# Two token blocks of the first layer by a Strassen form, and attention tiles turned by two VectorE transposes

## The chip, the cores and the metric

The kernel runs on one core of one Trainium2 chip. The metric is the device time of one execution in microseconds, the median of the runs.

## The reference

Attention in chunks of 64 tokens, then two feed-forward layers, all in float32 (cut to what matters):

```python
# q, k, v: (4, 8, 576, 64); chunks of 64 tokens that see only themselves
scores = matmul(q_c, k_c.T) / sqrt(64)
attn = exp(scores - max) / (sum + 1e-9)
x = (attn @ v_c), heads side by side          # (2304, 512)
h = x @ w_in1                                 # (2304, 2048)
g = softplus(h);   x = g @ w_out1             # (2304, 512)
h = x @ w_in2
g = (a0 + a1 h + a2 h^2 + a3 h^3) / (1 + |b0||h| + |b1| h^2 + 1e-6)
out = g @ w_out2
```

## The kernel before

**Number form.** A float32 product is made of three matmuls: each operand is split into a high part (rounded for the matmul, written by ScalarE or GpSimd) and a rest (`lo`, a subtraction on VectorE or GpSimd), and high x high, high x rest and rest x high are added in PSUM. The tuple `TERMS` holds the three. A weight tile or an x tile holds both parts, index 0 and 1.

**Tiles.** A *feature group* (`fc`) is 128 of the 2048 hidden features, 16 in all. A *block* is a set of tokens: layer one has 512, 512, 512, 384 and 384 (`BLOCKS`, blocks 0 to 4), layer two 512, 512, 512, 512 and 256. For one block and one group, `products_h` issues 12 matmuls (4 pieces of the 512 inputs x 3 terms) into a PSUM bank of `ps_h`, which has two; `softplus` (ScalarE twice, then the rest) or `rational` (six VectorE and five ScalarE instructions, and the rest on GpSimd) makes g, and `products_out1` or `products_out2` adds g times W_out into four banks for the whole block, 12 matmuls in two halves. The matmuls of h stand on L959, those of out on L1163 and L1196.

**Order of the blocks.** Layer one goes through blocks 0, 3, 4, 1, 2 (`ORDER1`), one group after another; layer two through 0, 3, 4, 1, 2 of its own.

**Attention.** A tile is 128 tokens, 18 in all. Seven are `STAGED` (0 to 3 and 12 to 14) and stand ready at the start in room that weights take later: PE turns q and k for them (`transpose`). The other eleven are loaded while layer one runs, with q and k in one tile of the pool `raw`, two transfers for most, and turned by 16 VectorE instructions of 32 partitions x 256 (`turn_blocks`, L655); their e is turned by 8 such instructions (`turn_e_blocks`, L759). PE adds 16 small matmuls for the scores (L677) and 16 for the values (L775). `finish_attention` lets the values of one tile go together with the scores of the next.

**Weights.** A 512 KB piece of a weight comes through SP's queue into `raw` (four buffers, shared with the attention), ScalarE and VectorE put it into float32 (`convert`: a scaling, a shift, one or two merges), and it is split into parts. Layer one's 32 pieces are converted during block 0. For layer two, 16 are converted early, stored to DRAM and loaded again (`reload_w`), and the `DIRECT` ones are converted when they are needed.

**Order of the work.** Every step is a task of `Program` with its engine, a cost, the tiles it reads and writes and the pool tags that it takes; the planner simulates these costs backward and forward, shakes the order and keeps the best one, and the program is written out in that order. Each engine then goes through its own instructions in order, SP through its transfers.

Of the kernel before, what the change touches and what calls it, by code (L numbers as in the profile page):

```python
# [20 lines left out]
P = 128  # L21
CH = 64
# [4 lines left out]
ORDER1 = (0, 3, 4, 1, 2)  # L27
# [4 lines left out]
DIRECT = range(2, 10)  # L32
# [6 lines left out]
APART = (0, 3)  # L39
PIECES = ((0, 256), (256, 256))  # L40
STAGED = (0, 1, 2, 3, 12, 13, 14)
QK_BY_VECTOR = {*range(4, 12), *range(15, 18)}
E_BY_VECTOR = {*range(4, 12), *range(15, 18)}


DIVIDE_BY_POOL = ()


FIRST_LOADS = "q0 k0 q1 k1 q2 k2 q3 k3 v0 v1 i0 v2 v3 i1 o0 q12".split()


class Program:
# [15 lines left out]
    def __init__(self):  # L68
        self.tasks, self.deps, self.table, self.port, self.psum = [], [], [], [], []
        self.writer, self.readers, self.last_alloc = {}, {}, {}  # L70
# [17 lines left out]
    def add(  # L88
# [22 lines left out]
        self.tasks.append((engine, cost, fn))  # L111
        self.deps.append(deps)
# [113 lines left out]
    def schedule(self):  # L226
# [7 lines left out]
        for seed in range(self.SEEDS):  # L234
# [48 lines left out]
def tile_chunk_attention_two_ffn(  # L283
# [72 lines left out]
    def on_dve(n, pointers=0):  # L356
        return 0.07 + 0.06 * pointers + n / 960

# [58 lines left out]
    def prepare(name, after, signed):  # L417
        layer, which, fc = name
        rkey = turn("raw", 4)
        spare = layer == 1 and turn("spare", 4)[1] == 3  # L420
# [84 lines left out]
    def reload_w(which, fc):  # L505
        if fc in DIRECT:
            convert(2, [(which, fc)], after=[steps[-1]])
            return
# [25 lines left out]

    loads = {}
# [5 lines left out]
    unfinished, done, begin = [], {}, {}  # L541

# [7 lines left out]
    def attention(tb):  # L550
# [13 lines left out]

        def load_qk(n):
# [3 lines left out]
            def f():  # L569
                if not staged and n == 0:  # L570
                    shape = [P, H, 2, D] if qk_by_vector else [P, 2, H, D]
                    qk_t[tb] = raw.tile(shape, F32, tag="raw", name=f"qk_{tb}")
                for off, m, b, s in runs(tb * TB, TB):
                    if not qk_by_vector:
# [4 lines left out]
                        continue  # L579
                    p0 = 64 * n + off // 2  # L580
                    sync.dma_start(
                        out=qk_t[tb][p0 : p0 + m // 2].rearrange("p h t d -> p h (t d)"),
                        in_=(q, k)[n][b, :, s : s + m, :].rearrange(
                            "h (p t) d -> p h (t d)", t=2
                        ),
                    )
# [3 lines left out]
        def load_v():  # L590
            if not staged:
                v_t[tb] = att1.tile([P, H, D], F32, tag="v", name=f"v_{tb}")
            for off, m, b, s in runs(tb * TB, TB):
# [54 lines left out]
        def turn_blocks(n, c, h, dq):  # L648


            def f():
                if (n, c, h, dq) == (0, 0, 0, 0):
                    new_turned()
                p0, p1 = 64 * h + 32 * dq, 64 * n + 32 * c
                vec.transpose(  # L655
                    tiles["qkT"][p0 : p0 + 32, n, :, c * CH : (c + 1) * CH].rearrange(
                        "p g (u t) -> p g t u", t=2
                    ),
                    qk_t[tb][p1 : p1 + 32, h::2, :, 32 * dq : 32 * dq + 32],
                )  # L660
# [3 lines left out]
        def scores():  # L664

            if qk_by_vector:
                new_ps()
            for n in range(16):
                g, c = (n // 4, n // 2 % 2) if by_chunk else (n // 8 * 2 + n // 2 % 2, n // 4 % 2)
# [825 lines left out]
```

## Time and profile before

| | |
|---|---|
| median of three runs (lowest, highest) | 842.61 us (842.59, 842.86) |
| span of the profiled execution | 842.7 us |
| PE busy | 832.9 us, 99% |
| VectorE, ScalarE, GpSimd busy | 639.7, 499.7, 226.0 us |
| chain that ended last | 97% PE |

The span is the time from the first to the last instruction of the one execution that was profiled; it stands beside the runs, which were not profiled. An engine's busy time says how much it did, the chain which of it was waited for. The granted clock is TensorE's, as a share of its full 2.4 GHz.

### The profile page before, as it was taken

The numbers are of one execution on the slowest core, as the hardware profiler recorded it, in microseconds if no ns is written. First come the engines' busy times: TensorE is split into PE (matmuls) and PEld (weight loads), VectorE is DVE, ScalarE is ACT, GpSimd is POOL, SyncE is SP. The second block draws the span as 40 slices with busy tenths as digits, with TensorE's granted clock in tenths as the row PEclk, the third lists the DMA queues.
The fourth block names the chain that finished last, engine by engine and source line by source line (L and its number), as shares of the span: only waits on it lengthen the run. The fifth ranks groups of instructions, "written<-read, shape, count | busy, mean of one in ns | idle before, by whom it ended". The sixth has DMA issues, their size and how long they took to land.

```text
span 842.7 us, 13146 instructions
## 1 busy us (share of the span) xinstructions
PE 832.9 (99%) x5020; PEld 714.7 (85%) x5020; DVE 639.7 (76%) x1125; ACT 499.7 (59%) x869; POOL 226.0 (27%) x206
## 2 busy tenths in 40 slices
PE   7999999999999999999999999999999999999998
PEld 6888889999999888888888888888889888888886
DVE  5788687887989887218887876868788886796785
ACT  5899962323335333244449766766778875676674
POOL 0000002222222121244355822322226261321312
PEclk9899999999999999999999999999999999999999
DMA  9965424214443713255434100200021000001001
GB/s 213 269 208 179 171 64 127 49 38 138 138 114 100 201 39 113 88 168 167 152 100 137 39 1 1 76 0 1 1 88 64 0 26 1 1 7 44 1 1 51
DMA packets 77984, 71.11 MB, mean 84 GB/s; under 512 B 36192, under 2 KB 65376, under 8 KB 77920
## 3 DMA queue, kind: packets, MB, share of 16 engines
q1 hardware_dynamic: 77920, 70.27, 28.8%
q8 instruction: 39, 0.64, 0.3%
q14 instruction: 25, 0.20, 0.1%
HBM read 56.63 MB, written 13.63 MB: 83 GB/s over the span
## 4 chain that ended last, share of the span: by engine, by line
PE 97%; SPq 2%; DMA 1%; ACT 0%; issue 0%
PE h L959 47%; PE acc L1163 24%; PE acc L1196 23%; PE aps L775 1%; SPq L575 1%; DMA wr_1i<-in_moe_w_in_dram 1%; PE aps L677 1%; PE h L984 1%; SPq L594 0%; SPq L427 0%; PE aps L630 0%; PE aps L746 0%; ACT cm_1i L446 0%; ACT ev_last L1262 0%; ACT room L768 0%
## 5 line engine op out<-in xcount | busy, mean ns | idle before, releaser
L1163 PE MATMUL acc<-g,w_1o 128*128 128x512 f32 (+1 forms) x960 | 210.9, 369 | 0.0
L959 PE MATMUL h<-xT,w_2i 128*128 128x512 f32 (+1 forms) x960 | 207.8, 368 | 0.0
L1196 PE MATMUL acc<-w_2o,g 128*128 128x512 f32 x864 | 206.6, 389 | 0.0
L959 PE MATMUL h<-xT,w_1i 128*128 128x512 f32 (+1 forms) x948 | 206.2, 368 | 0.0
L959 PEld LDWEIGHTS h<-xT,w_2i 128*128 128x128 f32 x960 | 168.9, 188 | 31.3 <-ACT u L1066 0.3
L1163 PEld LDWEIGHTS acc<-g,w_1o 128*128 128x128 f32 x960 | 174.1, 188 | 22.8
L959 PEld LDWEIGHTS h<-xT,w_1i 128*128 128x128 f32 x948 | 172.3, 188 | 22.2
L1196 PEld LDWEIGHTS acc<-w_2o,g 128*128 128x128 f32 x864 | 161.3, 188 | 32.8
L1034 POOL TENSOR_TENSOR g<-t,g 128x384 fp32r<-128x384 f32 (+1 forms) x64 | 76.5, 1196 | 325.8 <-ACT g L1031 325.8
L1099 POOL TENSOR_TENSOR g<-t,g 128x512 fp32r<-128x512 f32 (+1 forms) x80 | 94.6, 1183 | 253.6 <-ACT g L1096 169.2
L1026 ACT ACTIVATE t<-h 128x512 f32<-128x512 f32 (+1 forms) x80 | 44.5, 556 | 113.7 <-PE h L959 113.5
L1031 ACT ACTIVATE g<-h 128x512 fp32r<-128x512 f32 (+1 forms) x80 | 44.5, 556 | 73.4 <-PE acc L1163 71.8
L655 DVE STREAM_TRANSPOSE qkT<-qk 32x256 f32<-32x256 f32 x176 | 76.9, 437 | 12.0 <-PE aps L677 8.1
L1069 DVE SCALAR_TENSOR_TENSOR t<-u,absb_t,t 128x512 f32<-128x512 f32 (+1 forms) x80 | 55.5, 694 | 26.3 <-ACT u L1066 15.1
L1125 DVE TENSOR_TENSOR t<-h,t 128x512 f32<-128x512 f32 (+1 forms) x80 | 50.8, 636 | 31.5 <-ACT t L1084 14.4
L1114 ACT ACTIVATE t<-h,na_t 128x512 f32<-128x512 f32 (+1 forms) x80 | 58.6, 733 | 18.0 <-PE h L959 15.8
L1096 ACT ACTIVATE g<-t 128x512 fp32r<-128x512 f32 (+1 forms) x80 | 46.8, 585 | 37.7 <-DVE t L1069 34.6
L1069 DVE SCALAR_TENSOR_TENSOR t<-t,epsq_t,u 128x512 f32<-128x512 f32 (+1 forms) x80 | 55.3, 691 | 13.9 <-ACT u L1092 13.6
L1088 ACT ACTIVATE u<-t,epsq_t 128x512 f32<-128x512 f32 (+1 forms) x80 | 51.8, 648 | 22.6 <-DVE t L1069 20.5
L1069 DVE SCALAR_TENSOR_TENSOR t<-t,na_t,h 128x512 f32<-128x512 f32 (+1 forms) x80 | 55.5, 693 | 10.8 <-ACT t L1084 5.3
L1084 ACT ACTIVATE t<-h,b_t 128x512 f32<-128x512 f32 (+1 forms) x80 | 51.3, 641 | 16.8 <-PE h L959 10.1
L1069 DVE SCALAR_TENSOR_TENSOR u<-t,na_t,u 128x512 f32<-128x512 f32 (+1 forms) x80 | 55.6, 696 | 0.0
(86 smaller groups left out, 725.2 us busy)
## 6 DMA issues: line engine op xcount, KB each, us to landing
wr_1i<-in_moe_w_in_dram SPq DMA_DIRECT2D x16, 512.0 KB, 4.1
wr_1o<-in_moe_w_out_dram SPq DMA_DIRECT2D x16, 512.0 KB, 4.8
wr_2i<-in_moe_w_in_dram SPq DMA_DIRECT2D x16, 512.0 KB, 4.2
wr_2o<-in_moe_w_out_dram SPq DMA_DIRECT2D x16, 512.0 KB, 3.9
qk<-in_q_dram SPq DMA_DIRECT2D x16, 256.0 KB, 4.9
qk<-in_k_dram SPq DMA_DIRECT2D x16, 256.0 KB, 5.2
v<-in_v_dram SPq DMA_DIRECT2D x16, 256.0 KB, 5.0
out_dram<-ev SPq DMA_DIRECT2D x16, 256.0 KB, 2.5
```

The source lines that it names most:

```text
L655: vec.transpose(tiles["qkT"][p0 : p0 + 32, n, :, c * CH : (c + 1) * CH].rearrange("p g (u t) -> p g t u", t=2), qk_t[tb][p1 : p1 + 32, h:: ...
L959: pe.matmul(hs[s], w[:, a, c * P : (c + 1) * P], xt[:, b, c, :n_tok], start=n == 0, stop=n == 3 * KC - 1,)
L1034: (vec if by_vector else pool).tensor_tensor(out=gs[s][:, 1, :n_tok], in0=t["t2"], in1=gs[s][:, 0, :n_tok].bitcast(F32), op=ALU.subtract,)
L1069: return lambda: vec.scalar_tensor_tensor(out=out(), in0=in0(), scalar=scalar, in1=in1(), op0=op0, op1=op1)
L1084: act.activation(new("t1"), h(), AF.Abs, scale=b_t[:, 0:1])
L1088: act.activation(u(), d(), AF.Ln, bias=epsq_t)
L1096: act.activation(gs[s][:, 0, :n_tok], p(), AF.Copy)
L1099: pool.tensor_tensor(out=gs[s][:, 1, :n_tok], in0=p(), in1=gs[s][:, 0, :n_tok].bitcast(F32), op=ALU.subtract,)
L1114: lambda: act.activation(new("t2"), h(), AF.Identity, scale=na_t[:, 3:4], bias=na_t[:, 2:3]),
L1125: lambda: vec.tensor_tensor(out=p(), in0=h(), in1=p(), op=ALU.mult), [hkey, kp], [kp],
L1163: pe.matmul(accs[1, j, half][c % 2][:, :n_tok], wts[1, "o", fc][:, a, c * P : (c + 1) * P], gs[s][:, b, :n_tok], start=first and n == 0, s ...
L1196: pe.matmul(accs[2, j, half][c % 2], gs[s][:, b, c * P : (c + 1) * P], wts[2, "o", fc][:, a, :], start=first and n == 0, stop=last and n == 2,
```

## The change

**Order.** Layer one goes through blocks 0, 1, 2, and then through 3 and 4 together (`PAIR`). The staged tiles are 0 to 6; tile 7 comes during block 0, tiles 8 to 12 during block 1 and 13 to 17 during block 2.

**The pair.** For two feature groups f1, f2 and the two blocks a, b the four products h = x times W_in form a 2 x 2 matrix product, with the 512 inputs in halves: A11, A12 (group f1, inputs 0 to 255 and 256 to 511), A21, A22 (group f2), B11, B21 (block a) and B12, B22 (block b). `pair` forms S1 = A21 + A22, S2 = S1 - A11, S3 = A11 - A21, S4 = A12 - S2 on VectorE and splits them into parts; `turned_operands` and `turned_late` form, tile by tile, T1 = B12 - B11, T2 = B22 - T1, T3 = B22 - B12, T4 = T2 - B21. Seven products of 256 inputs (2 pieces x 3 terms = 6 matmuls) then stand where eight stood, with Winograd's order of sums: some of them in PSUM, where a later product goes on in a bank that ScalarE (`take`) or VectorE (`plus`) has read. Softplus of block a gives g as before; g of block b is kept in the room of used W_in tiles, and the out products of block b follow when all eight pairs are done.

**Attention.** q and k of a tile come in 16 transfers of 32 tokens x 8 heads x 32 values, so that one VectorE transpose of 128 x 512 turns q and one turns k (`turn_blocks`); v comes in four. GpSimd divides e for tiles 7 to 17.

**Weights of layer two.** `DIRECT` is 0 to 7; the reloads begin under block b's out products (`BACK`), and the direct ones are converted with one merge instead of two.

```diff
-ORDER1 = (0, 3, 4, 1, 2)
+ORDER1 = (0, 1, 2)
+PAIR = (3, 4)
-DIRECT = range(2, 10)
+DIRECT = range(0, 8)
-STAGED = (0, 1, 2, 3, 12, 13, 14)
+STAGED = tuple(range(7))
+BEGUN = (1, 5, 5)
+BEGIN_AT = ((9,), (0, 3, 6, 9, 13), (0, 2, 4, 7, 9))
+CONVERT = ((), (1, 2, 4, 5, 7, 8, 10, 11, 12, 14, 15), (1, 2, 3, 4, 5))
+BACK = (0, 0, 1, *(1,) * 13)
-DIVIDE_BY_POOL = ()
+DIVIDE_BY_POOL = range(7, 18)
+PAIR_BY_VECTOR = ("S24", "S1", "S3", "C12", "C22")
...
+                for c, b, s in chunks():
+                    for d0 in range(0, D, 32):
+                        for t0 in range(0, CH, 32):
+                            p0 = CH * c + d0
+                            sync.dma_start(
+                                out=qk_t[tb][p0 : p0 + 32, n, :, t0 : t0 + 32],
+                                in_=(q, k)[n][
+                                    b, :, s + t0 : s + t0 + 32, d0 : d0 + 32
+                                ].rearrange("h p d -> p h d"),
+                            )
...
-        def turn_blocks(n, c, h, dq):
+        def turn_blocks(n):
...
                 vec.transpose(
-                    tiles["qkT"][p0 : p0 + 32, n, :, c * CH : (c + 1) * CH].rearrange(
-                        "p g (u t) -> p g t u", t=2
-                    ),
-                    qk_t[tb][p1 : p1 + 32, h::2, :, 32 * dq : 32 * dq + 32],
+                    tiles["qkT"][:, n].rearrange("p g t -> p (g t)"),
+                    qk_t[tb][:, n].rearrange("p h t -> p (h t)"),
                 )
...
+    def turned_operands(part):
...
+            add(DVE, on_dve2(512), whole, [((xa, i), 0), ((xa, i), 1)], [ka], alloc="t1", port=True)
+            add(DVE, on_dve2(256), t3, [km], [kt], alloc="t1", port=True)
+            add(DVE, on_dve2(256), t1, [km, ka, kt], [km], port=True)
+            add(DVE, on_dve2(256), t2, [km, ka], [ka], port=True)
...
+    def pair(pi, s):
...
+        add(DVE, on_dve2(512), whole(f2), [(w2, 0), (w2, 1)], [k2], alloc="t1", port=True)
+        add(DVE, on_dve2(512), whole(f1), [(w1, 0), (w1, 1)], [k1], alloc="t1", port=True)
+        add(DVE, on_dve2(256), combine((f2, 1), (f2, 0), (f2, 1), ALU.add), [k2], [k2], port=True)
+        add(DVE, on_dve2(256), combine((f2, 0), (f1, 0), (f2, 0), ALU.subtract), [k1, k2], [k2], port=True)
+        add(DVE, on_dve2(256), combine((f1, 0), (f2, 1), (f1, 0), ALU.subtract), [k1, k2], [k1], port=True)
+        add(DVE, on_dve2(256), combine((f1, 1), (f1, 1), (f1, 0), ALU.subtract), [k1], [k1], port=True)
...
+        def product(a, b, n, new, start):
+            def f():
+                if new:
+                    new_bank(n)
+                for m, (i, j, c) in enumerate((i, j, c) for i, j in TERMS for c in range(2)):
+                    pe.matmul(
+                        banks[n], lhs(a, i, c), right(b, j, c),
+                        start=start and m == 0, stop=m == 5, skip_group_check=not start,
+                    )
...
+        def take(name):
...
+                act.activation(t[name], banks[0], AF.Copy)
...
+        def plus(name, k):
...
+                vec.tensor_tensor(out=t[name], in0=banks[1], in1=t[name], op=ALU.add)
...
+        product("A11", "B11", 0, True, True)
+        k11 = take("u1")
+        product("A12", "B21", 1, True, True)
+        plus("u1", k11)
+        g11 = activate("u1", k11, "A", f1, s + f1)
+        product("S2", "T2", 0, False, False)
+        k12 = take("u2")
+        product("S1", "T1", 1, False, True)
+        product("S3", "T3", 0, False, False)
+        k22 = take("u3")
+        plus("u3", k22)
+        product("A22", "T4", 0, False, False)
+        g21 = activate(None, None, "A", f2, s + f2)
+        product("S4", "B22", 1, False, False)
+        plus("u2", k12)
+        g12 = activate("u2", k12, "B", f1, s + FC + f1)
+        g22 = activate("u3", k22, "B", f2, s + FC + f2)
```

What this does to the order of the instructions is shown at three places. The first is PE in the stage of blocks 3 and 4. Before, in block 4, h of a group (12 matmuls into `h`) and the halves of out (into `acc`) take turns:

```order
L959 MATMUL h_36_2389<-xT_1693,w_1i_128 128x384 x12
L959 MATMUL h_37_2409<-xT_1693,w_1i_129 128x384 x12
L1163 MATMUL acc_4_1_0_2353<-g_2373,w_1o_648 128x384 x3
L1163 MATMUL acc_4_1_1_2354<-g_2373,w_1o_648 128x384 x3
L1163 MATMUL acc_4_0_2316<-g_2373,w_1o_648 128x384 x6
```

Now, in the fifth pair, the same place reads so (`p_0` and `p_1` are the pair's two banks; `s_4` holds S2 and S4, `S_4_3848` is S1, `S_4_3891` is S3; `T_0_3236` and `T_1_3237` are the two parts of T2, `T_0_3233` and `T_1_3234` those of T3; `xT_3366` holds T1):

```order
L1453 MATMUL p_0_3816<-T_1_3237,s_4_3921 128x384 x2
L1453 MATMUL p_0_3816<-T_0_3236,s_4_3921 128x384 x2
L1453 MATMUL p_1_3829<-xT_3366,S_4_3848 128x384 x6
L1453 MATMUL p_0_3816<-T_0_3233,S_4_3891 128x384 x2
L1453 MATMUL p_0_3816<-T_1_3234,S_4_3891 128x384 x2
```

Between S2 times T2 and S3 times T3, both into `p_0`, stands one group of six matmuls, S1 times T1; `take("u2")` on ScalarE reads `p_0` in that time.

The second place is SP's queue in the middle of block 0 (`wr_1i`, `wr_1o` are pieces of layer one's W_in and W_out). Before, weights alone stand there:

```order
L427 DMA wr_1i_863<-in_moe_w_in_dram 128x4x256
L432 DMA wr_1o_885<-in_moe_w_out_dram 128x1024
L427 DMA wr_1i_934<-in_moe_w_in_dram 128x4x256
L432 DMA wr_1o_983<-in_moe_w_out_dram 128x1024
L427 DMA wr_1i_1000<-in_moe_w_in_dram 128x4x256
```

Now q and k of tile 7 stand between them:

```order
L449 DMA wr_1i_920<-in_moe_w_in_dram 128x4x256
L454 DMA wr_1o_937<-in_moe_w_out_dram 128x1024
L618 DMA qk_949<-in_q_dram 32x8x32 x8
L618 DMA qk_949<-in_k_dram 32x8x32 x8
L449 DMA wr_1i_1027<-in_moe_w_in_dram 128x4x256
L454 DMA wr_1o_1038<-in_moe_w_out_dram 128x1024
```

The sixteen transfers moved ahead of the eleventh piece of W_in (`wr_1i_1027`).

The third place is VectorE where layer two begins (`h_80` is its first h, `cm_2i` and `cm_2o` are pieces of its weights in conversion). Before, the last direct piece is done when the first h comes:

```order
L393 TENSOR_TENSOR w_2o_4548<-cm_2o_4459,w_2o_4548 128x512
L1125 TENSOR_TENSOR t_80_4554<-h_80_4527,t_80_4554 128x512
L1069 SCALAR_TENSOR_TENSOR t_80_4576<-u_4562,absb_t,t_80_4576 128x512
L1069 SCALAR_TENSOR_TENSOR t_80_4554<-t_80_4554,na_t,h_80_4527 128x512
L1069 SCALAR_TENSOR_TENSOR t_80_4576<-t_80_4576,epsq_t,u_4562 128x512
```

Now conversions go on between the steps of the rational function:

```order
L483 SCALAR_TENSOR_TENSOR cm_2i_4615<-wr_2i_4571,cm_2i_4615 128x512
L1608 TENSOR_TENSOR t_80_4626<-h_80_4597,t_80_4626 128x512
L1553 SCALAR_TENSOR_TENSOR t_80_4642<-u_3483,row,t_80_4642 128x512
L415 TENSOR_TENSOR w_2i_4652<-cm_2i_4615,w_2i_4652 128x512
L483 SCALAR_TENSOR_TENSOR cm_2o_4629<-wr_2o_4594,cm_2o_4629 128x512
L1553 SCALAR_TENSOR_TENSOR t_80_4626<-t_80_4626,row,h_80_4597 128x512
```

The conversions moved from layer one's last block into the out products of block 4 and the first groups of layer two.

## Rows read from the trace of the kernel before

**Rows 1.** The page: engines' busy time, then the chain that ended last.

```profile
PE 832.9 (99%) x5020; PEld 714.7 (85%) x5020; DVE 639.7 (76%) x1125; ACT 499.7 (59%) x869; POOL 226.0 (27%) x206
...
PE 97%; SPq 2%; DMA 1%; ACT 0%; issue 0%
PE h L959 47%; PE acc L1163 24%; PE acc L1196 23%; PE aps L775 1%; SPq L575 1%; DMA wr_1i<-in_moe_w_in_dram 1%; PE aps L677 1%; PE h L984 1%; SPq L594 0%; SPq L427 0%; PE aps L630 0%; PE aps L746 0%; ACT cm_1i L446 0%; ACT ev_last L1262 0%; ACT room L768 0%
```

**Rows 2.** Waits of PE: who waited for whom, us in total, times, longest.

```profile
PE aps L746 <- DVE room L739: 2.4, 2, 1.9
...
PE aps L775 <- DMA v<-in_v_dram: 0.4, 1, 0.4
```

**Rows 3.** The chain in order of time: start us, us, what.

```profile
15.19 7.04 DMA wr_1i<-in_moe_w_in_dram
25.44 4.85 PE h L984 x24
...
37.27 2.95 PE h L959 x12
...
98.67 2.72 PE h L959 x12
...
183.12 4.16 PE h L959 x24
...
289.57 5.44 PE h L959 x24
...
823.84 14.97 PE acc L1196 x66
```

**Rows 4.** Stretches: length, then PE, PEld, DVE, ACT, POOL busy, granted clock, DMA.

```profile
0.00:20.00 20.00, 15.31 (x260) 13.10 (x260) 11.08 (x31) 10.68 (x18) 0.70 (x6) 0.98 1.06 203
...
80.00:120.00 40.00, 40.00 (x211) 33.29 (x210) 30.93 (x59) 36.05 (x53) 0.00 (x0) 1.00 0.42 132
112.00:245.00 133.00, 133.00 (x1120) 128.80 (x1119) 110.85 (x236) 45.33 (x86) 27.91 (x27) 1.00 0.35 91
...
420.00:507.00 87.00, 87.00 (x385) 72.03 (x385) 67.51 (x93) 59.45 (x102) 46.06 (x39) 1.00 0.22 67
507.00:594.00 87.00, 87.00 (x386) 72.03 (x385) 65.77 (x96) 59.86 (x101) 24.98 (x24) 1.00 0.05 19
```

**Rows 5.** Groups by line and shape: count, busy us, mean ns, idle before.

```profile
L655 DVE STREAM_TRANSPOSE qkT<-qk 32x256 f32<-32x256 f32 x176 | 76.9, 437 | 12.0 <-PE aps L677 8.1 <-DMA qk<-in_q_dram 0.6
...
L461 DVE SCALAR_TENSOR_TENSOR cm_2o<-wr_2o,cm_2o 128x512 uint32<-128x512 uint32 x32 | 27.2, 850 | 0.2
...
L393 DVE TENSOR_TENSOR w_1i<-cm_1i,w_1i 128x512 fp32r<-128x512 f32 x16 | 11.0, 687 | 0.8 <-ACT w_1i L385 0.6
...
L452 DVE TENSOR_SCALAR cm_2i<-cm_2i 128x512 uint32<-128x512 uint32 x16 | 10.6, 663 | 11.8 <-ACT cm_2i L448 11.5
...
L393 DVE TENSOR_TENSOR w_2o<-cm_2o,w_2o 128x512 fp32r<-128x512 f32 x8 | 8.8, 1094 | 1.3 <-POOL w_2o L387 1.3
...
L902 DVE TENSOR_TENSOR xT<-aps,xT 128x256 fp32r<-128x256 f32 x4 | 1.7, 416 | 0.0
...
L351 ACT ACT_TABLE_LOAD x25 | 32.1, 1283 | 1.2 <-PEq L1476 0.7
...
L1031 ACT ACTIVATE g<-h 128x384 fp32r<-128x384 f32 x32 | 15.7, 492 | 33.2 <-PE acc L1163 33.2
```

**Rows 6.** Timeline of PE and ScalarE: start us, us, instruction, idle before.

```profile
128.07 4.35 PE L959 MATMUL h<-xT,w_1i 128*128 128x384 f32 x24
...
130.37 0.49 ACT L1026 ACTIVATE t<-h 128x384 f32<-128x384 f32 x1 [0.57 <-PE h L959]
```

**Rows 7.** Timeline of SP and VectorE in block 0.

```profile
93.42 0.34 SPq L432 DMA_DIRECT2D wr_1o<-in_moe_w_out_dram  x1
...
94.73 0.69 DVE L393 TENSOR_TENSOR w_1i<-cm_1i,w_1i 128x512 fp32r<-128x512 f32 x1
...
98.80 0.37 SPq L427 DMA_DIRECT2D wr_1i<-in_moe_w_in_dram  x1
```

More of the change, by code (lines that the diff above doesn't have):

```diff
@@ L419, in prepare @@
         rkey = turn("raw", 4)
-        spare = layer == 1 and turn("spare", 4)[1] == 3
+        spare = layer == 1 and ("q", len(STAGED)) not in loads and turn("spare", 4)[1] == 3
         mkey = ("v", 0) if spare else turn("m", 3)
@@ L570, in f @@
                 if not staged and n == 0:
[L571 to L574, printed above, removed]
+                    qk_t[tb] = raw.tile([P, 2, H, D], F32, tag="raw", name=f"qk_{tb}")
+                if not qk_by_vector:
+                    for off, m, b, s in runs(tb * TB, TB):
                         sync.dma_start(
@@ L724, in exp, with bias, exp_by_head @@
                 act.activation(tiles["e"], tiles["e"], AF.Exp, scale=SCALE)
+        def bias():
+            tiles["nb"] = tiles["mx"]
+            vec.tensor_scalar(
+                out=tiles["nb"], in0=tiles["mx"], scalar1=-SCALE, scalar2=-FAR,
+                op0=ALU.mult, op1=ALU.add,
+            )
+        def exp_by_head():
+            tiles["far"] = True
+            tiles["e"] = new_e(0)
+            tiles["sm"] = small.tile([P, 8, 1], F32, tag="sm", name=f"sm_{tb}")
+            f = AF.Softplus if loaded[0] == SOFTPLUS else AF.Exp
+            for n in range(8):
+                act.activation(
+                    tiles["e"][:, n], ps[0][:, n // 4, n % 4 * CH : (n % 4 + 1) * CH], f,
+                    scale=SCALE, bias=tiles["nb"][:, n], accum_out=tiles["sm"][:, n],
+                )
         def total():
@@ L770, in values @@
         def values():
+            if by_chunk:
+                for n in range(16):
+                    c, g, y, h = n // 8, n // 4 % 2, n // 2 % 2, n % 2
+                    part_y, m, col = slice(y * CH, (y + 1) * CH), 4 * c + 2 * g + h, o0 + g * P
+                    pe.matmul(
+                        ps[0][CH * h : CH * h + CH, y, col + c * CH : col + (c + 1) * CH],
+                        v_t[tb][part_y, m],
+                        tiles["aT"][part_y, m],
+                        start=True,
+                        stop=True,
+                    )
+                return
             for g in range(4):
@@ L935, in finish, with keep @@
                 finish_first()
+                return
+            if j == PAIR[1]:
+                mk = bkey[part] = turn("m", 3)
+                def keep():
+                    b_t32[part] = cvt.tile([P, 512], F32, tag="m", name=f"xb_{part}")
+                    act.activation(
+                        b_t32[part].rearrange("p (b g t) -> p b g t", b=2, g=2),
+                        result(), AF.Copy,
+                    )
+                done[tb] = add(ACT, 0.52, keep, [b0, b1], [mk], alloc="m")
                 return
@@ L1053, in rational @@
         old = [("turned", "later", n) for n in range(16)] if third else []
-        u_keys = [("u", n) for n in range(2)]
         def u():
@@ L1060, in square @@
         def square():
-            if start:
-                att_stack.close()
-                ps_u = ctx.enter_context(tc.tile_pool(name="ps_u", bufs=1, space=PSUM))
-                for n in range(2):
-                    x["u", n] = ps_u.tile([P, 512], F32, tag=f"u{n}", name=f"u{n}")
             act.activation(u(), h(), AF.Square)
@@ L1211, in products_out2 @@
             )
+            if last and j == ORDER2[-1]:
+                prog.in_line([*ending, at])
+                ending[:] = [at]
+    ending = []
     x2d = [
@@ L1220, in evacuate @@
         name = layer, j, half
-        key = turn("raw", 4)
+        by_g = layer == 1 and j == ORDER1[-1]
+        key = turn("g", 2) if by_g else turn("raw", 4)
         for c in cs:
```

513 lines of the change are left out of this document (441 added, 72 removed).

## The prediction

> **What bounds the kernel now.** I read the shares of the engines and the chain of work that ended last first. PE is busy 832.9 us of 842.7, and 97% of the chain is PE, most of it on the three matmul lines (h, out of layer one, out of layer two) [rows 1]. PE waits only at the start: the two rows shown are the longest and the shortest of four, 5.7 us in all [rows 2]. The chain in order of time gives the rates [rows 3]: before 25.44 us it is start-up (the last of it a weight load, 7.04 us); from there one matmul follows another until 823.84 + 14.97 = 838.8 us, and 3.9 us of tail (last copy and store) are left. 24 matmuls of 512 columns take 5.44 us (0.2267 each), 24 of 384 columns take 4.16 (0.1733 each). In the stretches [rows 4] PE is busy 133.00 of 133 us and 87.00 of 87, at a granted clock of 1.00, while VectorE, ScalarE and GpSimd have room. So a matmul that is taken out shortens the run by its own rate, as long as the work put around it brings no wait; and an instruction taken from VectorE alone brings nothing.
>
> **The Strassen form, what it removes.** For a pair of feature groups and the two 384-token blocks, x times W_in took 2 x 2 x 12 = 48 matmuls of 384 columns; seven products of 6 are 42. Eight pairs: 384 become 336, and the built program has these counts. 48 x 0.1733 = 8.3 us. Every other matmul count is as before (layer one's out 576 and 384, layer two, 56 transposes and 28 in the turn of e, 288 + 288 small ones).
>
> **What it adds on VectorE.** Durations are [rows 5]: 0.687 us for 512 columns, 0.416 for 256; 384 lies between, I take 0.55. Per pair: two sums and one split rest of 512 (2.1), four combinations and two rests of 256 (2.5), three additions out of PSUM and two rests of 384 (2.8), together 7.3 us. PE's time per pair is 42 + 24 matmuls x 0.1733 = 11.4 us. It lies under PE with 4 us to spare; without that cover it would be 8 x 7.3 = 59 us.
>
> **On ScalarE.** Per pair three copies out of PSUM and eight softplus of 384 at 0.492, 5.4 us, and one 512 and two 256 columns of high parts, about 1.4 at the same rate: 6.8 of 11.4 us, 59% busy. Hidden too, but ScalarE now stands between two products of PE, which it did not before.
>
> **The hand-over, the new wait on PE.** Products 3 to 7 of a pair add to an accumulator that ScalarE or VectorE has to read first: 40 such places. In the order PE stands behind ScalarE's copy with only one group of 6 matmuls (1.04 us) between in 12 of them; the others have 2.08 or more. What one hand-over needs shows where ScalarE waits idle for h [rows 6]: the first twelve matmuls of the 24 that start at 128.07 are issued by 130.15 and ScalarE starts at 130.37, 0.22 later; with 0.49 for the copy that is 0.71 of the 1.04. The rest, 0.33, covers the next weight load, since a matmul group that had to wait shows 2.95 instead of 2.72 us [rows 3], 0.23 more. With ScalarE idle the price is nothing. With another instruction of 0.49 half done in front, the gap is passed by about 0.25. Bounds: 0, and 12 x (0.49 + 0.23) = 8.6 us. I take 12 x 0.59 (ScalarE's share) x 0.25 = 1.8 us, nearest to the low end, because the row has ScalarE start as soon as it may.
>
> **The turned operands and the attention.** Five tiles now fall on each of the two blocks of 87 us behind block 0, with 11 and 5 weight conversions and the sums for T1 to T4 (about 10 us). The transposes of q and k drop from 176 x 0.437 = 77 us to 22 of 128 x 512. No row shows one: between 0.437 (as long as the small ones) and twice that; I take 0.70, as other 512-column instructions, 15 us in all. VectorE per tile is then some 8 us, per block 40 + 30 of 87. That is 0.80; the stretch of the old run that held eight such tiles (112 to 245 us) shows VectorE at 110.85 of 133, 0.83, and PE without a gap [rows 4]. I put it at nothing, 0 to 1 us. The division on GpSimd (11 tiles) and T's rests fill an engine that is busy 27.91 of 133 there.
>
> **The queue of SP.** A tile's q and k come in 16 transfers instead of 2 (v in 4 instead of 1). One issue takes 0.37 us [rows 7], so 16 hold SP 5.9 us. Only tile 7 is loaded between layer one's weights, ahead of the eleventh piece of W_in; the weights queued behind it are what PE would wait for. They are ready 3.3 us ahead: the rest of the thirteenth W_in ends at 95.41, its h starts at 98.67 [rows 3, 7]. SP has nothing to issue from 93.8 to 98.8 there [rows 7], so the issues mostly fall into its own waits; I take 0, with 5.9 - 3.3 = 2.6 as the upper end. A tile's 512 KB are now pieces of 128 bytes, where they were 512. The row that comes nearest is the start, q, k and v in pieces of 256 bytes, 203 GB/s with the DMA engines full [rows 4]: about 2.5 us for a tile, under the 5.9 of the issues. The Trainium skill (DMA: Bandwidth & Descriptors, Specifications) wants at least 512 bytes for line rate, which speaks against this change; no run here shows pieces of 128 bytes. An estimate by it, half of 203 GB/s, makes a tile 5.1 us instead of 2.5, and the upper end here 5.2 instead of 2.6.
>
> **Start, block 0, tail.** Loads ahead of the first h are the same in kind and order, tile 4's in place of tile 12's. ScalarE (36.05 of 40 us in 80 to 120 [rows 4]) gains two table loads of 1.28 [rows 5] up to block 0's end and pays 1.2 for tile 7. Nothing, within 1 us either way. The tail keeps its order.
>
> **Sum.** Span 842.7 - 8.3 + 1.8 = 836.2; the median of the runs is 842.61, 0.1 below the span, so 836.1 us.
>
> **Rivals.**
> (W) Tile 7's transfers hold back the weights of block 0: +2.6, 838.7. For it the lead of only 3.3 us; against it SP's idle time.
> (V) VectorE becomes the bound at the turn to layer two. Fourteen of layer two's 32 weight pieces are asked for under block 4's out products and 18 under layer two's first block; before, 28 were under layer one's last block and 4 later. From the third out group to the ninth h of layer two PE has 13 x 2.08 + 9 x 2.72 + 5 x 2.72 = 65.1 us. VectorE has by the order 14.7 conversions, from 2.0 (0.663 and twice 0.687) to 2.6 us (0.663, 0.850, 1.094) [rows 5], 3.9 of splits and copies, and 40 instructions of the rational function at 65.77 / 96 = 0.685 [rows 4]: 60.7 to 69.5 us. At the upper end PE waits 4.4: 840.5. For it: no slack is sure. Against it: 420 to 507 had conversions beside the rational function, 67.51 of 87, and PE full.
> (H) The hand-over pays a whole ScalarE instruction in all 12 close places: +8.6 in place of 1.8, 842.9, no change.
> (S) Slower. All 40 dependent products, those behind VectorE's additions too, find their accumulator unread: 0.23 of weight load and half an instruction, 0.25, each, 19.2 us: 842.6 - 8.3 + 19.2 = 853.5. It decides from 0.21 us per place, where the gain is gone; from 0.25 it is slower. For it: seven products, two banks and three engines in a ring. Against it: 28 of 40 have 2.08 us or more.
> That the change doesn't do what it says, I leave without a chance: the matmuls are gone by count, and 384 columns have one rate.
>
> **How the numbers follow.** Forecast 0.63 (833.3 to 838.2: no loss and 1 us gained at the start, to twice the hand-over), W 0.08, V 0.12, H 0.09, S 0.08. About 0.2% is what a measurement here can tell from no change, 840.9 to 844.3. Faster: forecast, W, and three quarters of V, 0.80. Same: the rest of V and most of H, 0.11. Slower: S and a little of H, 0.09. The range that leaves out H and S goes from 833.3 to 841.0.
>
> **What would show it.** 336 matmuls of 384 columns on the products' line, at 0.173 each. In the pair stage (some 92 us) PE's waits on ScalarE's copies by name: a few of 0.1 to 0.4 us, 2 us together. Block 0's h groups as in the old chain, or 2 to 3 us of waits for w_1i behind tile 7 (W). The first h of layer two with VectorE near 95% and PE waiting for g (V). A span above 840 with PE full would say that the matmuls' rate changed; then the whole sum is wrong.

## The result, and the profile after

The changed kernel is a little slower, not faster. Its median is 848.4 us (847.66 to 849.12, four runs) against 842.74 us of the kernel before (842.59 to 843.1, four runs): a ratio of 1.0066, 95% interval 1.0052 to 1.0080. Forecast were 836.1 us. The profiled execution has a span of 847.3 us.

The page, first the engines, then the chain that ended last by engine (answers to [rows 1]):

```profile
PE 829.0 (98%) x4978; PEld 706.7 (83%) x4978; DVE 611.4 (72%) x1080; ACT 519.4 (61%) x927; POOL 224.2 (26%) x205
...
PE 86%; DVE 4%; DMA 4%; ACT 2%; SPq 2%; issue 1%; POOL 0%; ACTq 0%; POOLq 0%; DVEq 0%
```

The matmuls went as planned, x5020 to x4978: 48 fewer in the products and six more of `warm`. But PE is only 86% of the chain, where it was 97%; VectorE (4%), DMA (4%, before 1%) and ScalarE (2%) came in. PE's waits (who waited for whom: us in total, times, longest), where [rows 2] had none for h:

```profile
PE h L1065 <- ACT g L1137: 7.3, 3, 6.0
...
PE acc L1646 <- ACT g L1137: 0.8, 1, 0.8
PE acc L1646 <- DVE g L1140: 0.8, 2, 0.6
```

Stretches of the changed kernel, columns as in [rows 4]:

```profile
272.00:285.00 13.00, 6.96 (x77) 5.59 (x69) 7.19 (x11) 4.42 (x8) 1.81 (x1) 0.74 0.39 124
320.00:410.00 90.00, 89.86 (x513) 88.82 (x512) 54.61 (x111) 49.49 (x109) 15.68 (x16) 1.00 0.05 18
410.00:507.00 97.00, 96.89 (x477) 85.90 (x476) 78.83 (x125) 67.39 (x118) 34.42 (x31) 1.00 0.48 147
```

The Strassen stage (320 to 410) and the turn to layer two (410 to 507) are full: PE 89.86 of 90 and 96.89 of 97. The hole lies in the 13 us from 272 to 285 (PE 6.96 of 13), in block 2, before the pair begins. The timeline of PE shows it (start, us, instruction, in brackets the idle time before and its releaser):

```profile
272.17 0.65 PE L716 MATMUL aps<-qkT 64*64 64x64 f32 x32
278.86 4.69 PE L1065 MATMUL h<-xT,w_1i 128*128 128x512 f32 x12 [6.04 <-ACT g L1137]
```

PE waits for a softplus. ScalarE, in the same stretch, had stood idle for 11.82 us in front of an instruction that has nothing to do with it:

```profile
263.66 0.60 ACT L1137 ACTIVATE g<-h 128x512 fp32r<-128x512 f32 x1 [1.16 <-PE acc L1646]
276.08 0.66 ACT L470 ACTIVATE cm_2i<-wr_2i 128x512 f32<-128x512 f32 x1 [11.82 <-DMA w2o<-cm_2o]
277.26 1.06 ACT L1132 ACTIVATE t<-h 128x512 f32<-128x512 f32 x2
278.21 0.59 ACT L1137 ACTIVATE g<-h 128x512 fp32r<-128x512 f32 x1
```

The first step of converting a layer-two weight (`cm_2i`) needs one of three buffers of the tag `m`. It comes free when an earlier converted piece has been stored (`w2o<-cm_2o`), and ScalarE goes through its instructions in order, so the softplus behind it waits too. SP's timeline says why the store was late:

```profile
251.13 5.29 SPq L618 DMA_DIRECT2D qk<-in_q_dram  x8
256.51 4.91 SPq L618 DMA_DIRECT2D qk<-in_k_dram  x8
261.52 3.85 SPq L618 DMA_DIRECT2D qk<-in_q_dram  x8
265.47 2.58 SPq L633 DMA_DIRECT2D v<-in_v_dram  x4
268.09 4.06 SPq L618 DMA_DIRECT2D qk<-in_k_dram  x8
272.19 0.46 SPq L523 DMA_DIRECT2D w2o<-cm_2o  x1
```

From 251.13 to 272.15 SP issues nothing but small transfers of tiles, 36 of them, one behind the other; then come the stores. The first is issued at 272.19, and ScalarE goes on at 276.08. After the hole TensorE's clock is low for a while:

```profile
272.80:278.80 6.00, 0.02 (x3) 0.00 (x0) 1.84 (x4) 2.72 (x6) 0.00 (x0) 0.74 0.40 139
278.80:282.40 3.60, 3.54 (x8) 2.81 (x9) 3.60 (x5) 0.50 (x2) 1.81 (x1) 0.50 0.26 96
282.40:290.00 7.60, 7.60 (x35) 6.25 (x34) 5.38 (x13) 1.81 (x3) 2.33 (x2) 1.00 0.22 59
```

PE had been idle for 6 us; then the granted clock is 0.50 (the level of 1.2 GHz) for 3.6 us and 1.00 again. The first twelve matmuls take 4.69 us where twelve take 2.72 in [rows 3]; 1.6 us of that is the clock.

So the theory was: **Q**, the 20 small transfers of a tile fill SP's in-order queue, what stands behind them (weights, stores) comes late, ScalarE waits for it in order and PE waits for ScalarE. The price, by how much later the matmul behind each wait begins, is 6.1 us here (of which the row above shows 6.04 as idle time), two like it of 0.94 and 0.66 us at 243 and 172 us (behind weight loads `wr_2i` that came late), and 1.6 us of clock: 9.3 us. Rivals: **P**, the pieces of 128 bytes fill the DMA engines; **O**, the new order of work on ScalarE and the Strassen stage lose the time, whatever the loads do.

### The profile page after: what moved, and what is told of

Its sections match the earlier page's. It is cut to its first block, busy times and chain, and to the rows that moved or that the text cites. A ratio compares the mean times of both kernels' runs of the same rounds, so it can differ in the third digit from the quotient of the medians.

```text
span 847.3 us, 13413 instructions
## 1 busy us (share of the span) xinstructions
PE 829.0 (98%) x4978; PEld 706.7 (83%) x4978; DVE 611.4 (72%) x1080; ACT 519.4 (61%) x927; POOL 224.2 (26%) x205
## 4 chain that ended last, share of the span: by engine, by line
PE 86%; DVE 4%; DMA 4%; ACT 2%; SPq 2%; issue 1%; POOL 0%; ACTq 0%; POOLq 0%; DVEq 0%
PE h L1065 34%; PE acc L1679 23%; PE acc L1646 20%; PE u L1453 3%; PE p L1453 3%; SPq L618 1%; DMA wr_1o<-in_moe_w_out_dram 1%; DMA wr_2i<-in_moe_w_in_dram 1%; PE warm L1982 1%; DMA qk<-in_k_dram 1%; DMA qk<-in_q_dram 1%; PE aps L845 1%; PE aps L677 1%; SPq L633 1%; DVE t L1553 0%
## 5 line engine op out<-in xcount | busy, mean ns | idle before, releaser
L1065 PE MATMUL h<-xT,w_1i 128*128 128x512 f32 x564 | 137.4, 395 | 7.3 <-ACT g L1137 7.3
L1065 PEld LDWEIGHTS h<-xT,w_1i 128*128 128x128 f32 x564 | 106.3, 190 | 30.6 <-ACT g L1137 8.3
L1597 ACT ACTIVATE t<-h,row 128x512 f32<-128x512 f32 (+1 forms) x80 | 58.7, 733 | 24.3 <-PE h L1065 23.8
L1140 POOL TENSOR_TENSOR g<-t,g 128x512 fp32r<-128x512 f32 x32 | 43.2, 1350 | 103.0 <-ACT g L1137 101.8
L1553 DVE SCALAR_TENSOR_TENSOR t<-t,row,u 128x512 f32<-128x512 f32 (+1 forms) x80 | 55.2, 691 | 19.6 <-ACT u L1576 19.0
L1572 ACT ACTIVATE u<-t,row 128x512 f32<-128x512 f32 (+1 forms) x80 | 51.8, 648 | 25.0 <-DVE t L1553 24.3
L1553 DVE SCALAR_TENSOR_TENSOR t<-t,row,h 128x512 f32<-128x512 f32 (+1 forms) x80 | 55.3, 692 | 12.9 <-ACT u L1550 5.7
L1568 ACT ACTIVATE t<-h,row 128x512 f32<-128x512 f32 (+1 forms) x80 | 51.2, 642 | 17.1 <-PE h L1065 9.8
L1553 DVE SCALAR_TENSOR_TENSOR t<-u,row,t 128x512 f32<-128x512 f32 (+1 forms) x80 | 55.3, 693 | 6.0 <-ACT u L1550 5.8
L1553 DVE SCALAR_TENSOR_TENSOR u<-t,row,u 128x512 f32<-128x512 f32 (+1 forms) x80 | 55.5, 695 | 0.0
L1550 ACT ACTIVATE u<-h 128x512 f32<-128x512 f32 (+1 forms) x80 | 43.3, 542 | 14.9 <-DVE t L1608 9.7
```

Of the source, the lines that this page charges most:

```text
L1065: pe.matmul(hs[s], w[:, a, c * P : (c + 1) * P], xt[:, b, c, :n_tok], start=n == 0, stop=n == 3 * KC - 1,)
L1550: act.activation(u(), h(), AF.Square)
L1553: return lambda: vec.scalar_tensor_tensor(out=out(), in0=in0(), scalar=scalar, in1=in1(), op0=op0, op1=op1)
L1568: act.activation(new("t1"), h(), AF.Abs, scale=b_t[:, 0:1])
L1572: act.activation(u(), d(), AF.Ln, bias=epsq_t)
L1597: lambda: act.activation(new("t2"), h(), AF.Identity, scale=na_t[:, 3:4], bias=na_t[:, 2:3]),
```

## The experiments

Each ran in one group with fresh runs of the kernel before, whose median was 842.76 to 842.98 us; the ratio stands against those.

| run | median us | ratio to before, 95% |
|---|---|---|
| few issues | 839.05 | 0.9956 (0.9943 to 0.9970) |
| big pieces | 846.43 | 1.0046 (1.0033 to 1.0059) |
| half the issues | 838.60 | 0.9950 (0.9938 to 0.9962) |
| Strassen alone | 852.68 | 1.0117 (1.0103 to 1.0131) |
| transposes alone | 843.54 | 1.0011 (1.0002 to 1.0019) |
| stores on GpSimd's queue | 839.06 | 0.9957 (0.9944 to 0.9971) |
| weights on GpSimd's queue | 842.18 | 0.9992 (0.9979 to 1.0005) |
| few issues, and stores on GpSimd | 838.80 | 0.9958 (0.9943 to 0.9972) |
| the kernel before, stores on GpSimd | 842.75 | 1.0000 (0.9991 to 1.0010) |
| stores first, same plan | 842.46 | 0.9996 (0.9987 to 1.0005) |
| honest costs, new plan | 844.25 | 1.0018 (1.0010 to 1.0027) |
| honest costs and weights on GpSimd | 844.31 | 1.0020 (1.0009 to 1.0031) |
| stores early, new plan | 846.13 | 1.0042 (1.0027 to 1.0057) |
| stores on GpSimd, new plan | 847.78 | 1.0043 (1.0016 to 1.0070) |

### Fewer issues, or bigger pieces

Same plan and order as the changed kernel; only how q, k (and v) are brought differs. These two runs, and later half the issues and few issues with the stores moved, bring as many bytes as the changed kernel but leave out the right data of q or k (with few issues of v too).

```diff
-        for d0 in range(0, D, 32):            # few issues
-            for t0 in range(0, CH, 32):
-                sync.dma_start(out=qk_t[tb][p0:p0+32, n, :, t0:t0+32], ...)
+    for off, m, b, s in runs(tb * TB, TB):
+        sync.dma_start(out=qk_t[tb][off:off+m, n], ...)   # v likewise
```
```diff
-                    out=qk_t[tb][p0:p0+32, n, :, t0:t0+32], ...  # big pieces
+                    out=qk_t[tb][p0:p0+32, n, h0:h0+4] as "p (h d)", in_ 4 whole tokens a row
```

> Leaves the right data of q, k and v out: each tile of blocks 1 and 2 (tiles 7 to 17) brings the same bytes in 1 or 2 transfers each for q, k and v, in pieces of 256 bytes, instead of 8, 8 and 4; every engine's order is that of the changed kernel, only SP issues less. Theory Q (SP's queue: the issues of the small transfers, 0.45 to 0.65 us each, keep the loads and stores of layer two's weights waiting, ScalarE waits in its order for them and PE for a softplus behind): PE's three waits for g at 171.75, 243.10 and 271.66 us go (0.66 + 0.94 + 6.12) and the low clock behind the last (1.6), 9.3 us: 848.4 - 9.3 = 839.1. Theory P (the 128-byte pieces fill the DMA engines): half the packets are left, 842 to 846. Theory O (the order of ScalarE or the Strassen stage loses the time, whatever the loads do): 848.

> Leaves the right data of q and k out: each of the 16 transfers of a tile moves as many bytes as in the changed kernel, in pieces of 1 KB instead of 128 bytes; the order and the number of issues are those of the changed kernel. Theory Q (the number of issues): no change, 847.5 to 849. Theory P (the 128-byte pieces): PE's waits for g go, 839. Theory O: 848.

Few issues: 839.05, as Q said (839.1). Big pieces: 846.43, 2.0 less than the changed kernel. Q had said no change, which is a miss: the size of the pieces counts for something, a fifth of the 9.3. But PE still waits 5.1 us for g there, so most of the loss goes with the issues. PE, ScalarE and the other engines in blocks 1 and 2 (112 to 320 us), first in the changed kernel, then with few issues:

```profile
112.00:320.00 208.00, 200.68 (x1486) 163.60 (x1485) 129.17 (x248) 72.29 (x129) 56.98 (x46) 0.98 0.44 109
```
```profile
112.00:320.00 208.00, 208.00 (x1538) 171.75 (x1537) 139.36 (x265) 77.36 (x139) 58.03 (x47) 1.00 0.39 112
```

PE is full, and the share of the DMA engines was under half in both. P as the main cause is out, and so is O as the cause of the 9.3 us: the same orders, the same pair, and the loss is gone.

### One half of the change at a time

"Strassen alone" takes `load_qk`, `load_v`, `turn_blocks`, `scores` and `values` from the kernel before and keeps block order, pair and planner; "transposes alone" puts the new ones into the kernel before. Both are planned anew.

> The changed kernel with q, k and v loaded, turned and multiplied as in the kernel before (2 transfers of q and k in pieces of 512 bytes, sixteen VectorE transposes a tile); block order, Strassen pair and planner as changed, its plan made anew. Theory Q: matmuls -8.3, hand-over +0.9, turn to layer two +0.7, start +2: 838; VectorE has 11 x (77/11 - 1.4) = 61 us more in the 174 us of blocks 1 and 2, where it was busy 0.62, so it comes to 0.97 and PE may wait for it: up to 846. Waits on VectorE's qkT or g there, not on wr_2i. Theory O: PE's wait of 6 us for ScalarE's g stays, 848.

> The kernel before, with its block order and no Strassen form, but q and k in 16 transfers and two transposes a tile, v in 4. Theory Q: four tiles fall on a block of 66 to 87 us, SP issues 4 x 10.5 us beside the conversions' loads and stores (12 us): the queue is full for stretches of 20 to 30 us and ScalarE's conversions come late: 844 to 850. Theory O: the loads do no harm, 842.7, or a little less.

Strassen alone is the slowest of all, 852.68 and not up to 846, a miss. The 6 us wait is gone, as Q said. VectorE is busier, 182.14 us of the 208 from 112 to 320 where the changed kernel had 129.17, but blocks 1 and 2 themselves lose nothing: from 128 to 300 us PE is full with VectorE at 153.93 of 172. The loss sits at the two ends (the stretches 128 to 300 and 312 to 338, then waits of PE from 100 to 340):

```profile
128.00:300.00 172.00, 172.00 (x1284) 141.14 (x1283) 153.93 (x323) 57.85 (x98) 49.34 (x39) 1.00 0.45 126
312.00:338.00 26.00, 20.15 (x120) 17.25 (x119) 21.50 (x46) 9.13 (x22) 4.03 (x4) 0.93 0.10 40
```
```profile
PE acc L1616 <- DVE g L1110: 2.3, 3, 1.7
PE acc L1616 <- POOL g L1475: 1.6, 1, 1.6
PE acc L1616 <- ACT g L1466: 1.3, 1, 1.3
PE p L1423 <- ACT u L1444: 1.2, 2, 0.6
PE aps L829 <- DVE aT L813: 1.0, 1, 1.0
```

The waits for `g L1110` lie at the end of block 0, where the chain runs through the 16 transposes of tile 7 among the weight conversions. The other four lie where the pair begins: the chain there goes through the eight small transposes of the last tile's e, then the sums for T1 to T4, to a g that comes late. So in this plan the old transposes do cost, through VectorE, at the two places where other VectorE work is due at once; that five tiles a block are too much for VectorE is not shown, and neither is that every plan would lose so much.

Transposes alone is 843.54, 0.1% slower than before, where Q had said 844 to 850: a miss. The same 220 small transfers go through SP there, and PE is busy 208.00 of 208. The longest run of them in the queue is even longer, 52 from 106.39 to 135.65, but layer two's weights are not yet in work, and behind the run stands a store of x:

```profile
131.74 3.91 SPq L588 DMA_DIRECT2D qk<-in_k_dram  x8
135.74 0.40 SPq L1283 DMA_DIRECT2D x<-ev  x1
```

Where those weights are loaded and stored, from 188 us on, at most 20 small transfers stand in a row. ScalarE waits for `wr_2i` 3.2 us in all, against 16.2 and the 11.8 in the changed kernel (first transposes alone, then the changed kernel, both 112 to 320 us):

```profile
ACT cm_2i L448 <- DMA wr_2i<-in_moe_w_in_dram: 3.2, 2, 3.0
```
```profile
ACT cm_2i L470 <- DMA wr_2i<-in_moe_w_in_dram: 16.2, 5, 5.3
ACT cm_2i L470 <- DMA w2o<-cm_2o: 11.8, 1, 11.8
```

A full queue is not enough, then, and neither is a long run of small issues. What costs is such a run with something behind it that an in-order engine needs next.

### What stands behind the small transfers

```diff
-                sync.dma_start(out=w2d[name], in_=x["m", name])
+                nc.gpsimd.dma_start(out=w2d[name], in_=x["m", name])   # 16 stores
```

The orders of PE, VectorE and ScalarE are those of the changed kernel. "Weights on GpSimd's queue" moves the 16 loads of those weights too.

> The changed kernel, order of PE, VectorE and ScalarE unchanged, with the 16 stores of layer two's converted weights issued from GpSimd's queue instead of SP's; q, k, v as in the changed kernel, SP's number of small issues too. Theory Q (what costs is that the store, and so the buffer ScalarE's conversion waits for, stands behind the small issues in SP's queue): the 6.1 us wait at 272 us, which ends with a store w2o from cm_2o, goes with its low clock (1.6); the waits behind late loads wr_2i (0.94 and 0.66) stay: 848.4 - 7.7 = 840.7; up to 843 if GpSimd's issues delay its divisions. If it is the stretch itself (SP's small issues slow q and k, whatever stands behind them): 848.

> As the run with the stores on GpSimd's queue, with the 16 loads of those weights (wr_2i, wr_2o in blocks 1 and 2) there too. Theory Q: all three waits of PE for ScalarE's g go, 848.4 - 9.3 = 839.1, as with few issues; GpSimd, which waits in order for a free buffer at each load, may hold back a division: up to 845. If the small issues cost by themselves: 848.

> The kernel before with the 16 stores of layer two's converted weights issued from GpSimd's queue, nothing else. Theory Q: SP's queue holds nothing back there, PE has no wait, so no change, 842.6 to 843.2. If moving the stores were a gain by itself, whatever the change: 838 to 841.

> Leaves the right data of q, k and v out as in the run with few issues, and the stores go through GpSimd's queue: both reliefs at once, every other order that of the changed kernel. If they take away one and the same wait (theory Q): 839, as each alone. If the small issues and the stores cost separately: 834 to 836.

The 16 stores alone give the loss back: 839.06. The stores behind the old hole are issued from 263.74 on instead of 272.19; ScalarE's wait shrinks from 11.82 to 4.41 us, which PE has room for (GpSimd's timeline, then ScalarE's, then the stretch from 262 to 285). One wait of PE for g is left in blocks 1 and 2 of that profile, 1.2 us at 240 us, behind late weight loads, as the theory had it:

```profile
263.74 0.58 POOL L523 DMA_DIRECT2D w2o<-cm_2o  x1
```
```profile
266.34 0.67 ACT L470 ACTIVATE cm_2i<-wr_2i 128x512 f32<-128x512 f32 x1 [4.41 <-DMA w2o<-cm_2o]
```
```profile
262.00:285.00 23.00, 23.00 (x219) 18.76 (x218) 17.00 (x38) 7.12 (x12) 10.08 (x11) 1.00 0.41 105
```

In the kernel before, the same edit changes nothing (1.0000), so it is no gain by itself. With few issues as well it is 838.80: the two reliefs take away one and the same loss. That the loads in GpSimd's queue too make it worse (842.18, its runs spread from 840.1 to 845.4) fits with GpSimd's in-order waits at a load, but its profiled run was one of the short ones and shows no wait of PE over 0.4 us in blocks 1 and 2, so I leave that open.

### The place of the stores, and the number of issues

"Stores first" keeps the plan, and in SP's queue alone puts each store in front of the tiles' transfers as soon as its data exist; "half the issues" brings k in 1 or 2 transfers and leaves q and v as changed.

```diff
+            if i in small_loads:                       # stores first
+                for m in stores:
+                    if m not in given and given.issuperset(prog.deps[m]):
+                        emitted.append(m)
```
```diff
+                if n == 1:                             # half the issues: k as in few issues
```

> The changed kernel's plan, the order of PE, VectorE, ScalarE and GpSimd word for word; only in SP's queue each store of a converted weight is put in front of the tiles' transfers as soon as what it stores has been computed in that order. All 20 transfers a tile stay, all on SP. Theory Q in its narrow form (the store's place behind the small transfers): the wait of 6 us goes, 839 to 841. If the queue is simply too full and the next in it (a tile's q and k) is then waited for: 844 to 848.

> Leaves the right data of k out: k of tiles 7 to 17 in 1 or 2 transfers in pieces of 256 bytes, q in its 8 and v in its 4 as in the changed kernel; every order that of the changed kernel. SP has some 4 us less to issue per tile, 8 us less in the stretch before the stall, which is more than the 6.1 us that PE waited: by theory Q the stall goes at once, 839 to 841. If the gain goes with the number of issues: half of 9.3, 843.7.

Stores first: 842.46, between the two forecasts. The 11.82 us wait is gone (SP, then ScalarE):

```profile
253.17 0.38 SPq L526 DMA_DIRECT2D w2o<-cm_2o  x1
```
```profile
265.83 0.66 ACT L473 ACTIVATE cm_2i<-wr_2i 128x512 f32<-128x512 f32 x1
```

but what now stands behind is late: weight loads, and the tiles' own chains (ScalarE, then PE's waits). The load that ScalarE waits 8.75 us for is issued at 178.08, behind 20 small transfers and a store:

```profile
184.57 0.66 ACT L473 ACTIVATE cm_2i<-wr_2i 128x512 f32<-128x512 f32 x1 [8.75 <-DMA wr_2i<-in_moe_w_in_dram]
```
```profile
PE h L1068 <- ACT g L1140: 2.0, 2, 1.0
PE aps L848 <- DVE aT L832: 0.8, 1, 0.8
```

The order in the queue brings back 5.9 of 9.3 us, and the rest needs less in the queue. Half the issues: 838.60, the whole loss at once, as Q said. The store that ScalarE had waited for and those behind it are then issued by 259.35, and ScalarE does not wait (SP, then ScalarE):

```profile
258.87 0.48 SPq L523 DMA_DIRECT2D w2o<-cm_2o  x1
```
```profile
261.40 0.67 ACT L470 ACTIVATE cm_2i<-wr_2i 128x512 f32<-128x512 f32 x1
```

### The planner told of it

The planner's cost of a tile's q or k load was 2.8 us and of v 1.4; the rows show 3.9 to 5.3 and 2.6.

```diff
-                DMA, 2.8 if qk_by_vector else 1.2, load_qk(n), [],      # honest
+                DMA, 4.4 if qk_by_vector else 1.2, load_qk(n), [],
-            add(DMA, 1.4, load_v, ...)
+            add(DMA, 2.6, load_v, ...)
```
```diff
+            prog.lead = 20.0                                            # stores early
             add(DMA, 0.95, store, [mkey], [("w2d", name)])
```
```diff
-            add(DMA, 0.95, store, [mkey], [("w2d", name)])              # stores on GpSimd, new plan
+            add(POOL, 0.6, store, [mkey], [("w2d", name)])
```

> The changed kernel with the planner told what the traces show for SP: 4.4 us for the 8 transfers of a tile's q or k (it had 2.8) and 2.6 for the 4 of v (1.4). The plan is made anew, nothing else changes. Theory Q: the planner puts the weights' loads and stores in front of tiles where it can; 839 to 843. If SP is simply full in blocks 1 and 2 (5 x 10.5 + 11 x 1.5 = 70 of 87 us), the planner can't help and 846 to 850 is left. Theory O: 848.

> Both: the planner's costs of the traces, and layer two's converted weights loaded and stored through GpSimd's queue. Theory Q: 838 to 841, as the better of the two alone; if GpSimd's in-order waits at the loads cost, 842 to 846.

> The changed kernel, all transfers in SP's queue, with the planner told to place each store of a converted weight 20 us ahead of its due time; the plan is made anew. The stores w2o, w2i that stood behind two tiles of q and k now stand in front of the second. Theory Q (the place of the store in the queue): the wait of 6 us goes, 839 to 843. If the queue has to be relieved of issues: 846 to 850.

> The stores on GpSimd's queue with the planner told of it (0.6 us of GpSimd each, nothing of the DMA queue); the plan is made anew. Theory Q: 837 to 841, like the stores moved in the emitted order alone; a new plan can cost 1 to 5 us elsewhere, as the one with honest costs did.

Honest costs: 844.25, outside the 839 to 843 of Q. The hole is gone (in blocks 1 and 2 PE waits 0.7 us for g and 0.8 for a weight), but the new plan loses elsewhere, in block 0 and in the pair, where PE waits for ScalarE:

```profile
PE p L1453 <- ACT S L1411: 1.4, 1, 1.4
```

With the weights on GpSimd's queue the plan, and the loss, are the same: 844.31. The two others are misses. In "stores early" the store is in time, and ScalarE stands 8.10 us before the exponential of a tile whose k, the last of its transfers, was issued at 272.05, in the same stretch:

```profile
276.16 0.72 ACT L776 ACTIVATE e<-e,row 128x512 f32<-128x512 f32 x1 [8.10 <-DVE e L766]
```

"Stores on GpSimd, new plan" has its hole at 270 us, two waits of 2.8 us together, where the chain of a tile holds PE itself; its runs went from 842.7 to 849.1, so its median says little. In both, SP issues 36 small transfers between 250 and 274 us again, almost one behind the other. Relief by a new plan thus depends on the plan. The stores moved in the written-out program, with the old plan, are the best version found that brings all the data: 839.06, 0.43% under the kernel before and 1.1% under the changed one.

## Why the prediction was wrong, point by point

**The step that failed is "The queue of SP".** It worked out that 16 issues hold SP for 5.9 us a tile, and then asked only for tile 7 in block 0, the one tile among layer one's weights, and put the term at 0 to 2.6. The ten tiles of blocks 1 and 2 were costed under "The turned operands and the attention" for VectorE alone, 0 to 1 us. With its own 0.37 us [rows 7], 5 tiles of 20 transfers are 37 us of issues in 87 us, in one queue with 11 conversions' loads and stores; the rows show 0.45 us for an issue of q or k and 0.61 for v:

```profile
261.96 0.45 SPq L618
...
266.77 0.61 SPq L633
```

The question it did not ask was what stands behind those issues and which engine waits for it in order. Measured: 9.3 us, 848.4 - 839.06, and the same by few issues (9.3) and half the issues (9.8). The row of 0.37 us was a fifth too low, but that was not the fault: a queue that the change fills in three blocks was looked at in one. Where it was looked at, the term of 0 was right: block 0 takes as long with tile 7's transfers whole (stores moved) as with few of them. The sentence on pieces of 128 bytes was weighed as a bandwidth for tile 7: the run with big pieces shows 2.0 us for them over all eleven tiles, less than a quarter of the loss.

**The Strassen form was right.** 48 matmuls of 384 columns are gone. A chain of the changed kernel in the pair stage reads

```profile
332.18 2.08 PE p L1453 x12
334.26 1.04 PE acc L1646 x6
```

which is 0.173 per matmul, the rate of [rows 3]: -8.3 us.

**The hand-over was right in kind, and smaller than its term.** To see where time goes I take the *lag* of a matmul: its start less the sum of all matmuls before it at full rate (0.2267, 0.1733, 0.12, 0.111 and 0.02 us for 512, 384, 256, 128 and 64 columns; `warm` counts as nothing). A lag that grows is time lost on PE.

| lag of PE, us | kernel before | changed | stores moved | half the issues |
|---|---|---|---|---|
| first h of 512 columns | 16.8 | 15.8 | 14.5 | 15.5 |
| end of block 0 | 17.8 | 19.8 | 17.8 | 18.8 |
| first product of the pair | | 30.0 | 19.8 | 19.4 |
| last product of the pair | | 30.5 | 20.4 | 19.9 |
| end of layer one | 18.4 | 30.7 | 20.6 | 20.1 |
| last matmul | 18.8 | 32.0 | 21.9 | 21.3 |

Over the pair stage the lag grows by 0.5 us in all three (forecast 1.8), and no wait of PE on a copy is listed there. H and S are out, and V too: from the pair's end to the last matmul it grows by 1.5, against 0.4 in layer two before. VectorE in the stage is busy 54.61 of 90 us (0.61; forecast 7.3 of 11.4, 0.64), ScalarE 49.49 (0.55; forecast 0.59).

**The transposes were right.** Forecast 0.70 us, measured (group by shape):

```profile
L701 DVE STREAM_TRANSPOSE qkT<-qk 128x512 f32<-128x512 f32 x22 | 15.5, 706 | 19.7 <-DMA qk<-in_k_dram 12.4 <-DMA qk<-in_q_dram 6.6 <-issue 0.5
```

The idle time at its end is the queue again: VectorE waits for q and k, as did the chains above.

**Block 0 was mis-sized.** Forecast for the start and block 0: nothing, within 1 us. The start is not worse. Within block 0 the lag grows by 3.9 us in the changed kernel and by 3.3 with the stores moved or half the issues, where the kernel before has 1.0 (1.6 with its stores moved). In the changed kernel PE waits there for g:

```profile
34.40 0.50 PE L1646 MATMUL acc<-g,w_1o 128*128 128x512 f32 x1 [0.83 <-ACT g L1137]
...
109.62 2.56 PE L1646 MATMUL acc<-g,w_1o 128*128 128x512 f32 x10 [0.58 <-DVE g L1140]
```

A table load of ScalarE stands shortly before each (at 31.97 and 105.60). But the two loads more that the prediction counted are not in the trace (21 in the whole run, where [rows 5] has 25), so their number is not the cause. It comes with the new plan, not with tile 7's transfers; no run was made to find it, and it stays open.

**The sum.** Between the two profiled executions, changed less before: -8.3 (matmuls) - 1.0 (start) + 3.0 (block 0) + 9.5 (blocks 1 and 2, the queue) + 0.5 (pair) + 1.1 (turn and layer two) = +4.8; the spans differ by 4.6, the medians by 5.7. The start of first matmuls differs by up to 2 us between runs of one plan, so its term may be noise. Without the queue, half of the 8.3 is left: the run with the stores moved is 3.9 under the before of its group (842.98). The starting point was loose too: every run's time lies about 1.8 us over its span, and the profiled span of 842.7 is among the longest of the kernel before, whose later runs have 840.3 to 842.8; the two nearly cancelled, so taking 0.1 us between span and median did no harm. The upper end of the forecast's own range, twice the hand-over, is 837.9 and not 838.2, which changes nothing.

**The rivals and the signs.** W had the right mechanism (tiles' transfers hold back weights) at the wrong place and with a quarter of the price; 0.08 for it and 0.09 for "slower" were too little, since no rival was built on blocks 1 and 2. The sentence that a span above 840 with PE full would speak for another rate did not apply: PE was not full.

## What to carry to other kernels

When a change multiplies small transfers, add up the issues per stage against the stage's length, find the longest run of them in the queue's order, and ask of each thing behind it which in-order engine needs it next: here stores that nobody reads for some 200 us held a buffer, the buffer a conversion, the conversion a softplus, and that PE. A few transfers that free a buffer may be better on a queue of their own: here that gave back the whole loss, while a place ahead of the bulk loads gave back 5.9 of 9.3 us. A planner that is given 2.8 us for what takes 4 to 5 can place such a store just in time, and it will be late.

## What the runs showed of the hardware

An issue on SP costs by the transfer, hardly by its bytes. Medians in the changed kernel: 0.45 us for 32 KB of q or k in 256 pieces, 0.61 for 64 KB of v, 0.39 for a store of 256 KB. The Trainium skill (DMA: Bandwidth & Descriptors, Issuing engines are not separate DMA queues) says that issuing from several engines only saves the time to initiate a transfer, "usually small relative to the DMA itself". Here one issue is small beside the 3.0 us in which a transfer of q lands, but the 20 issues of a tile, 9.6 us, are not. And what a second queue saved was less the 16 issues it took over (16 x 0.39 = 6.2 us of SP) than their place behind others: 9.3 us on PE's path, and nothing in the kernel before, where the same 16 moved.

The loss does not go by the count of issues: seven fewer for most tiles (half the issues) give the same as seventeen fewer (few issues), within half a microsecond. And PE's hole of 6 us comes with 1.6 us of matmuls at the lower clock, 0.50, on top.
